# Weight rounding in four evenly dealt pieces, weight sums on VectorE, and another product order

## The chip, the cores and the metric

The kernel runs on one core of one Trainium2 chip. TensorE (PE in the profile) does the matrix products, VectorE (DVE) and ScalarE (ACT) the work on single elements, GpSimd (POOL) a little of it and the stores, and SyncE (SP) issues the loads. The metric is the device time of one execution in microseconds.

## What is computed

Attention inside chunks of 64 tokens, then a gated layer, then a layer with a rational function. All matrices are 32-bit floats.

```python
scores = scale * q_c @ k_c.T; attn = softmax(scores)        # 4 x 8 heads, 9 chunks of 64, head size 64
x = (attn @ v_c).reshape(2304, 512)
y = ((x @ w_a) * (x @ w_b)) @ w_out                          # 512 -> 1536 -> 512
h = y @ w_in
P = a[0] + a[1] * h + a[2] * h * h + a[3] * h * h * h
Q = 1 + abs(b[0]) * abs(h) + abs(b[1]) * h * h
out = (P / (Q + 1e-6)) @ w_out2                              # 512 -> 2048 -> 512
```

## The kernel before

**Numbers in two parts.** A matrix product takes both operands as a high and a low part: `mm3` (line 226) multiplies high by high, high by low and low by high into one place of PSUM. So every operand has to be split first: ACT rounds it to the high part, DVE subtracts to get the low one. For weights the split is longer, because a weight is first rounded in a particular way. `w_front` (line 187) takes a raw weight tile of 128x512 and makes a term c with two DVE instructions (lines 199, 200) and a term z with two ACT instructions (lines 201, 202). `w_next` (line 205) adds them on DVE (line 216), then `w_put` makes the high part on ACT (line 184) and, one call later through `w_flush`, the low part on DVE (line 185). That is four DVE and three ACT instructions for each tile. There are 24 tiles of w_a and w_b, 12 of w_out, and 32 of w_in and w_out2. `w_fetch` (line 154) loads them, `AHEAD` = 5 tiles early in the first stage and 2 early later.

**The order.** The order of every engine's instructions is that in which the Python code calls them; each engine works its own list from the front, and an instruction that waits holds all behind it. A list `todo` with due times (`later`, `tick`, line 245) strews the attention's pieces between the products.

**A start** (to 26.6 us): the attention of the first three units of 128 tokens, in an order written by hand (`FIRST`, `LOADS`, lines 80 and 83).

**The first stage** (26.6 to 200.1 us): `ab_half` (line 460) forms x @ w_a and x @ w_b of the first 768 tokens, 24 pairs (`seq`, line 784) of two times 12 products of 384 columns, 576 in all. Between them stand the attention of the other 15 units and the weights: `w_more` (line 792) makes one or no weight after each half pair. A unit's softmax (`a_soft`, line 345 ends it) is followed by a transposition on PE (line 353). After six units `x_second` (line 410) makes the differences that the second stage needs, on POOL (lines 399 and 417).

**The second stage** (200.1 to 432.9 us): x @ w_a and x @ w_b of the other 1536 tokens with seven instead of eight block products. `s_prep` (line 488) makes the sums of the weights for a tile i of 12: it takes the rounded weights back from memory (`s_load`, line 481, one buffer `wf`), forms four sums on POOL (line 512) and splits on ACT and DVE (lines 503 and 507). `s_step` (line 538) runs one tile over 768 tokens, 24 steps of 42 products of 384 columns. A step's order on PE is product 1, 2, then 7 of the step before, 5, 6, then 3 of the step before, then 4. After product 7 ACT copies y (`s_snap`, line 535), DVE forms `b` from it and from the sum q (line 576), and only then may product 3 add to q.

**The third stage** (432.9 to 623.4 us): `y_part` (line 614) multiplies with w_out, 60 places of 12 products: 12 places of 256 columns and 48 of 512. `g_fetch` loads a place's operand two places ahead, `g_parts` (line 608) splits it one place ahead (ACT line 116, DVE line 117). The 32 weights of the last stage are rounded here too, by `w_next` behind each place.

**The fourth stage** (623.4 us to the end): the layer with the rational function, `step2`.

Of the kernel before, what the change touches and what calls it, by code (L numbers as in the profile page):

```python
# [11 lines left out]
I32 = mybir.dt.int32  # L12
# [8 lines left out]
def chunk_attention_two_mlps(  # L21
# [104 lines left out]
    p_qk = phase.enter_context(tc.tile_pool(name="qk", bufs=2, side="right"))  # L126
    p_t = phase.enter_context(tc.tile_pool(name="t", bufs=5, side="right"))
# [20 lines left out]
    raws = {}  # L148

    n_cv = [0, 0, len(order1)]  # L150
    pend_w = []
    front_w = []
# [29 lines left out]
    def w_put(key, x):  # L182
        wt[key] = hi, lo = w_tile(key, F32R)
        nc.scalar.copy(hi, x)
        return lambda: nc.vector.tensor_tensor(lo, x, hi.bitcast(F32), ALU.subtract)  # L185

    def w_front():

        while n_cv[0] < n_cv[2] and n_cv[0] < n_cv[1] + (AHEAD if n_cv[0] < len(order1) else 2):
            w_fetch()  # L190
        if n_cv[1] == n_cv[2]:
            return
        t = raws.pop(order[n_cv[1]])
# [3 lines left out]
        c, z = w_tile(order[n_cv[1]], I32)  # L197
        zz = z.bitcast(F16).rearrange("p (f t) -> p f t", t=2)
        nc.vector.tensor_scalar(c.bitcast(F32), hw.bitcast(F32), 2.0 ** -112, None, ALU.mult)
        nc.vector.tensor_scalar(c, c, 3, None, ALU.logical_shift_left)  # L200
        nc.scalar.activation(zz[:, :, 1], hw.bitcast(F32), AF.Copy, scale=2.0 ** -112)  # L201
        nc.scalar.activation(zz[:, :, 0].bitcast(U16), lw, AF.Copy, scale=2.0 ** -13)  # L202
        front_w.append((c, z))

    def w_next(n):


        for _ in range(min(n, n_cv[2] - n_cv[1])):
            if not front_w:
                w_front()  # L210
            c, z = front_w.pop()
            key = order[n_cv[1]]
            n_cv[1] += 1
            x = p_io.tile([P, DM], I32, name="w_x", tag="io")
            w_flush()
# [3 lines left out]
            pend_w.append(w_put(key, x.bitcast(F32)))  # L219
            w_front()  # L220

    def w_flush():
        if pend_w:
            pend_w.pop()()
# [235 lines left out]
    def ab_half(i, h, nm):  # L460
        ps = ps_acc.tile([P, GH], F32, name="ab", tag="acc")
        for kk in range(KD):
            if kk == KD // 2:
                tick(0.5)
# [14 lines left out]
    wf = {}  # L479

    def s_load(i):

        t = p_j2.tile([P, 4, 2 * P], F32, name="wf", tag="wf")
# [4 lines left out]
    def s_prep(i):  # L488
# [4 lines left out]
        n = 2 * P  # L493

        p = p_j2 if i % 2 == 0 else p_j1
        made = {}

        def hi(nm, at, m, products):
            def f():
                t = made[nm] = (p if nm in "ab" else p_j1).tile([P, 2, m], F32R, name="ws_" + nm, tag=f"ws_{nm}{i % 2}")  # L500
# [29 lines left out]
    def s_tile(name):  # L530
        return p_j1.tile([P, GH], F32, name=name, tag=name, bufs=2)
# [6 lines left out]
    def s_step(i, g, prev, fill):  # L538
# [18 lines left out]
        if i is not None:  # L557
# [5 lines left out]
            fill()  # L563
        last()
# [43 lines left out]
    def g_parts(j, i):  # L608
        hi = p_g.tile([P, SIZES[j]], F32R, name="g_hi", tag="g_hi")
        lo = p_g.tile([P, SIZES[j]], F32R, name="g_lo", tag="g_lo")  # L610
        split(hi, lo, raw.pop(("g", j, i)))
        g1[j, i] = (hi, lo)

# [151 lines left out]
    for item in FIRST:  # L765
        if item in "fwl":
            w_front() if item == "f" else w_flush() if item == "l" else w_next(1)
            continue
# [15 lines left out]
    seq = [(i, h) for h in range(2) for i in range(3)] + [(i, h) for i in range(3, F1) for h in range(2)]  # L784
    for n in range(UH):
        a_unit(UH + n, 0.5 * n, (0, 0.5, 1, 1.5, 2, 3, 4))
    FROM, PER, GAP = 5.5, 3.0, 2.0
    for n in range((NQ - 1) * 2 * UH):
        a_unit(2 * UH + n, FROM + PER * n + (GAP if n >= 2 * UH else 0), (0, 0.5, 2, 3, 3.5, 5, 6.5))
    slot = 0  # L790
    for n, (i, h) in enumerate(seq):
        def w_more():
            due = min(slot + 3, 6) if slot < 6 else slot // 2 + 4
            if min(due, len(order1)) > n_cv[1]:
                w_next(min(due, len(order1)) - n_cv[1])
            else:
                w_flush()

# [3 lines left out]
        w_more()  # L802
        tick(0.5)
        slot += 1
        ps_b = ab_half(i, h, "b")
        if n == len(seq) - 1:
            break
        gated(i, h, a_s, ps_b)
        w_more()
        tick(0.5)  # L810
        slot += 1
    w_flush()
    phase.close()

    p_j1 = phase.enter_context(tc.tile_pool(name="j1", bufs=1, side="right", reuse_waits="tile"))
# [114 lines left out]
```

## Time and profile before

| | us |
|---|---|
| median of 3 runs | 1020.22 (1019.73 to 1023.4) |
| the profiled execution's own time | 1022.57 |
| its span in the trace | 1020.8 |
| PE busy | 932.6 (91%) |
| DVE busy | 725.3 (71%) |
| ACT busy | 590.5 (58%) |
| POOL busy | 143.8 (14%) |

The page gives each engine's busy time, the granted clock of TensorE in slices of the span, the groups of instructions with what ended the idle time ahead of them, and the DMA issues. A matmul's end is modelled, so its listed length overlaps the next one; how fast products really follow each other is read from their starts. The mean granted clock over the span is 0.958 of full speed.

### The profile page before, as it was taken

The page shows a single profiled execution, that of the slowest core. Times are in us where ns is not written, and L with a number is a line of the kernel's source. Part 1 is how long each engine was busy: PE and PEld are TensorE (multiplying, and loading weights), DVE is VectorE, ACT ScalarE, POOL GpSimd, SP SyncE. Part 2 cuts the span into 40 slices and gives each one's busy share as a digit, 9 for nine tenths or more (in the row PEclk, how much of TensorE's full clock was granted, in tenths as well). Part 3 has the DMA queues.
Part 4 walks back from the last instruction along what each step waited for, and adds up shares of the span by engine and source line. Part 5 has one row for each costly group of instructions (what it writes and reads, how often), then busy time and mean ns, then how long its engine had stood idle before and what let it go on. Part 6 is the DMA issues. An engine that isn't in the chain of part 4 may idle for free.

```text
span 1020.8 us, 14783 instructions
## 1 busy us (share of the span) xinstructions
PE 932.6 (91%) x5516; PEld 812.7 (80%) x5516; DVE 725.3 (71%) x1286; ACT 590.5 (58%) x1070; POOL 143.8 (14%) x192
## 2 busy tenths in 40 slices
PE   6689979978888799968999989999999999999998
PEld 5579978868888699866666669988888888888897
DVE  5567868545547576646556555999988988898896
ACT  5456756334223343335555546888767766776775
POOL 0011363372232232200000000000000000000000
PEclk9789989979789999989999999999999999999999
DMA  9948866223222323265666552002002000200100
GB/s 231 247 131 251 243 172 157 73 78 132 90 81 80 120 90 117 72 200 183 206 204 218 205 175 83 1 1 73 0 1 83 1 1 1 73 1 1 42 1 31
DMA packets 107335, 105.82 MB, mean 104 GB/s; under 512 B 61440, under 2 KB 84480, under 8 KB 107264
## 3 DMA queue, kind: packets, MB, share of 16 engines
q1 hardware_dynamic: 99264, 79.71, 27.1%
q0 software_dynamic: 8000, 25.17, 6.8%
q8 instruction: 43, 0.70, 0.3%
q14 instruction: 28, 0.23, 0.1%
HBM read 74.98 MB, written 29.88 MB: 103 GB/s over the span
## 4 chain that ended last, share of the span: by engine, by line
PE 44%; ACT 5%; DVE 3%; issue 2%; DMA 1%; ACTq 0%; SPq 0%
PE acc L229 8%; PE acc L230 8%; PE acc L228 8%; PE h L230 6%; PE h L228 6%; PE h L229 6%; ACT g_hi L116 1%; DVE g_lo L117 1%; DVE w_x L216 1%; DMA g_raw<-g_d 1%; ACT w_i L201 1%; ACT w_i L202 1%; DVE w_o L185 1%; ACT w_o L201 1%; DVE w_i L185 1%
## 5 line engine op out<-in xcount | busy, mean ns | idle before, releaser
L230 PE MATMUL h<-y,w_i 128*128 128x512 f32 (+1 forms) x320 | 117.8, 368 | 0.0
L228 PE MATMUL h<-y,w_i 128*128 128x512 f32 (+1 forms) x320 | 117.8, 368 | 0.0
L229 PE MATMUL h<-y,w_i 128*128 128x512 f32 (+1 forms) x320 | 117.7, 368 | 0.0
L228 PE MATMUL acc<-g_hi,w_o 128*128 128x512 f32 (+1 forms) x240 | 93.4, 389 | 16.7 <-ACT g_hi L116 16.7
L229 PE MATMUL acc<-g_lo,w_o 128*128 128x512 f32 (+1 forms) x240 | 93.8, 391 | 5.7 <-DVE g_lo L117 5.3
L677 ACT ACTIVATE a_ring<-h 128x512 f32<-128x512 f32 (+1 forms) x80 | 44.1, 551 | 89.3 <-PE h L230 89.3
L230 PE MATMUL acc<-g_hi,w_o 128*128 128x512 f32 (+1 forms) x240 | 91.4, 381 | 0.0
L117 DVE TENSOR_TENSOR g_lo<-g_raw,g_hi 128x512 fp32r<-128x512 f32 (+1 forms) x60 | 37.8, 638 | 73.0 <-ACT g_hi L116 72.8
L680 DVE SCALAR_TENSOR_TENSOR u<-u,cb_t,a_ring 128x512 f32<-128x512 f32 (+1 forms) x80 | 55.7, 696 | 31.2 <-ACT u L678 30.4
L229 PE MATMUL acc<-w_o,g_hi 128*128 128x512 f32 x191 | 75.2, 394 | 0.0
L228 PE MATMUL acc<-w_o,g_hi 128*128 128x512 f32 x191 | 74.8, 392 | 0.0
L230 PE MATMUL acc<-w_o,g_lo 128*128 128x512 f32 x191 | 74.2, 388 | 0.0
L228 PEld LDWEIGHTS acc<-g_hi,w_o 128*128 128x128 f32 x240 | 47.2, 197 | 31.4 <-ACT g_hi L116 23.4
L535 ACT COPY s<-y 128x384 f32<-128x384 f32 x72 | 34.1, 476 | 64.8 <-PE y L230 63.9
L470 POOL DMA_DIRECT2D g_d<-g x72 | 39.6, 550 | 224.4 <-DVE g L579 93.5
L228 PEld LDWEIGHTS h<-y,w_i 128*128 128x128 f32 x320 | 60.1, 188 | 9.0
L229 PEld LDWEIGHTS h<-y,w_i 128*128 128x128 f32 x320 | 60.1, 188 | 8.7
L230 PEld LDWEIGHTS h<-y,w_i 128*128 128x128 f32 x320 | 60.0, 188 | 7.5
L229 PEld LDWEIGHTS acc<-g_lo,w_o 128*128 128x128 f32 x240 | 47.2, 197 | 20.8 <-DVE g_lo L117 12.8
L228 PE MATMUL q<-xs,ws 128*128 128x384 f32 x96 | 36.1, 377 | 25.6 <-DVE b L576 25.4
L679 ACT ACTIVATE t<-h,ca_t 128x512 f32<-128x512 f32 (+1 forms) x80 | 59.0, 738 | 0.0
L682 DVE SCALAR_TENSOR_TENSOR t<-t,ca_t,h 128x512 f32<-128x512 f32 (+1 forms) x80 | 55.6, 694 | 2.8
(167 smaller groups left out, 2563.1 us busy)
## 6 DMA issues: line engine op xcount, KB each, us to landing
w_raw<-in_moe_w_out_dram SPq DMA_DIRECT2D x28, 512.0 KB, 3.8
g_d<-g POOLq DMA_DIRECT2D x72, 192.0 KB, 2.2
g_raw<-g_d SPq DMA_DIRECT2D x48, 256.0 KB, 3.9
w_raw<-in_moe_w_in_dram SPq DMA_DIRECT2D x16, 512.0 KB, 3.8
w_raw<-in_moe_w_a_dram SPq DMA_DIRECT2D x12, 512.0 KB, 6.0
w_raw<-in_moe_w_b_dram SPq DMA_DIRECT2D x12, 512.0 KB, 5.7
out_dram<-o SPq DMA_DIRECT2D x18, 256.0 KB, 2.4
y_d<-ys POOLq DMA_DIRECT2D x16, 256.0 KB, 4.2
```

What stands on the lines that cost most here:

```text
L117: nc.vector.tensor_tensor(lo, x, hi.bitcast(F32), ALU.subtract)
L185: return lambda: nc.vector.tensor_tensor(lo, x, hi.bitcast(F32), ALU.subtract)
L201: nc.scalar.activation(zz[:, :, 1], hw.bitcast(F32), AF.Copy, scale=2.0 ** -112)
L228: nc.tensor.matmul(ps, wh, xh, start=first, stop=False, **kw)
L229: nc.tensor.matmul(ps, wh, xl, start=False, stop=False, **kw)
L230: nc.tensor.matmul(ps, wl, xh, start=False, stop=last, **kw)
L470: nc.gpsimd.dma_start(out=g_d[i][:, tok:tok + GH], in_=g)
L535: nc.scalar.copy(t, ps)
L677: nc.scalar.activation(ah, ps, AF.Abs)
L679: nc.scalar.activation(t, ps, AF.Identity, scale=ca_t[:, 3:4], bias=ca_t[:, 2:3])
L680: nc.vector.scalar_tensor_tensor(u, u, cb_t[:, 0:1], ah, ALU.add, ALU.mult)
L682: nc.vector.scalar_tensor_tensor(t, t, ca_t[:, 1:2], ps, ALU.add, ALU.mult)
```

## The change

**Weights.** `w_front`, `w_next` and `w_put` become `w_piece`: four pieces, each with one DVE instruction and, save the last, one ACT instruction; a weight's high part is made in the second piece of the next weight and its low part in the third. `w_until` is called at every half of a product group (`half`), so the pieces come two at a time at first and then singly; in the second stage about 2.3 stand in each step; in the third stage `g_parts` hands back its DVE instruction, which is issued behind the first piece. One weight fewer is loaded ahead.

**Sums.** The four sums of each tile move from POOL to DVE. `wf` gets two buffers and is loaded two tiles ahead. The sums of tiles 0 and 1 are loaded, and those of tile 0 made, within the first stage (`s_begin`, at due time `END`), whose attention units follow each other a little faster. The split sums lie in the space of x and of the raw weights, which are free by then.

**Products.** Product 4 of a step stands ahead of product 3 of the step before.

```diff
     FIRST = (
-        "k0 d2 q0 k1 q1 S0 X0 d4 S1 X1 k2 E0 f q2 E1 P0 S2 V0 d2 P1 X2 L0 w V1 E2 k3 q3 l L1 d2 P2 V2 L2 w"
+        "k0 d2 q0 k1 q1 S0 X0 d4 S1 X1 k2 E0 w w q2 E1 P0 S2 w w V0 d2 P1 X2 L0 w w V1 E2 w w L1 d2 P2 w w V2 L2 w"
     ).split()
-    LOADS = "k0 q0 k1 q1 w v0 k2 q2 w v1 v2 w k3 q3 w k4 q4 v3 w k5 q5 v4 v5".split()
-
-    AHEAD = 5
+    LOADS = "k0 q0 k1 q1 w v0 k2 q2 w v1 v2 w k3 q3 w k4 q4 v3 k5 q5 v4 v5".split()
+
+    AHEAD = 4
...
+        if piece == 0:
+            nc.scalar.activation(zz[:, :, 1], hw.bitcast(F32), AF.Copy, scale=2.0 ** -112)
+            nc.vector.tensor_scalar(c.bitcast(F32), hw.bitcast(F32), 2.0 ** -112, None, ALU.mult)
+        elif piece == 1:
+            w_hi(n - 1)
+            nc.vector.tensor_scalar(c, c, 3, None, ALU.logical_shift_left)
+        elif piece == 2:
+            nc.scalar.activation(zz[:, :, 0].bitcast(U16), lw, AF.Copy, scale=2.0 ** -13)
+            w_lo(n - 1)
+            w_fetch_ahead(n + 1)
+        else:
+            del terms[n]
+            x = f32s[n] = p_io.tile([P, DM], I32, name="w_x", tag="io")
             nc.vector.tensor_tensor(x, c, z, ALU.add)
...
-        t = p_j2.tile([P, 4, 2 * P], F32, name="wf", tag="wf")
+        t = p_j2.tile([P, 4, 2 * P], F32, name="wf", tag="wf", bufs=2)
...
         def add(o, x, y, op):
-            return lambda: nc.gpsimd.tensor_tensor(f[:, o], f[:, x], f[:, y], op)
+            return lambda: nc.vector.tensor_tensor(f[:, o], f[:, x], f[:, y], op)
 
         return [
-            hi("a", 0, 2 * n, (1, 2)), lo("a", 0, 2 * n), hi("b", 3 * n, n, (4,)), lo("b", 3 * n, n),
+            hi("a", 0, 2 * n, (1, 2)), hi("b", 3 * n, n, (4,)), lo("a", 0, 2 * n), lo("b", 3 * n, n),
             add(3, 2, 3, ALU.add), add(2, 0, 2, ALU.subtract), add(0, 3, 0, ALU.subtract),
-            hi("2", 2 * n, 2 * n, (7, 5)), lo("2", 2 * n, 2 * n), add(1, 1, 0, ALU.subtract),
-            hi("1", 0, 2 * n, (6, 3)), lo("1", 0, 2 * n),
+            hi("2", 2 * n, 2 * n, (7, 5)), add(1, 1, 0, ALU.subtract), hi("1", 0, 2 * n, (6, 3)),
+            lo("2", 2 * n, 2 * n), lo("1", 0, 2 * n),
         ]
...
             s2 = s_snap(y, "s2")
             fill()
+            r = ps_ab.tile([P, GH], F32, name="r", tag="ab"[n % 2])
+            s_product(r, i, g, 4, True)
+            fill()
         last()
         fill()
         if i is None:
             return None
-        r = ps_ab.tile([P, GH], F32, name="r", tag="ab"[n % 2])
-        s_product(r, i, g, 4, True)
-        fill()
...
-    seq = [(i, h) for h in range(2) for i in range(3)] + [(i, h) for i in range(3, F1) for h in range(2)]
+    seq = [(i, h) for h in range(2) for i in range(4)] + [(i, h) for i in range(4, F1) for h in range(2)]
     for n in range(UH):
-        a_unit(UH + n, 0.5 * n, (0, 0.5, 1, 1.5, 2, 3, 4))
-    FROM, PER, GAP = 5.5, 3.0, 2.0
+        a_unit(UH + n, 1.0 + 0.5 * n, (0, 0.5, 1.5, 2, 2.5, 3.5, 4.5))
+    FROM, PER, GAP = 6.0, 2.75, 1.0
...
+    def s_begin():
+
+        nonlocal p_j2
+        s_t.close()
+        p_j2 = s_t.enter_context(tc.tile_pool(name="j2", bufs=1, side="right", reuse_waits="tile"))
+        s_load(0)
+        s_load(1)
+
+    def s_do(t, op):
+        if op == 0:
+            preps[t] = s_prep(t)
+        preps[t][op]()
+        if op == 11 and t + 2 < F1:
+            s_load(t + 2)
+
+    END = math.ceil(2 * (FROM + PER * ((NQ - 1) * 2 * UH - 1) + GAP + times[-1] + 0.25)) / 2
+    todo.append((END, n_todo[0], s_begin))
...
+        n = n_half[0]
+        n_half[0] += 1
+        w_until(min(11 + 2 * n, 32) / 4 if n < 17 else (n + 18) / 4)
...
     for n, (j, i) in enumerate(places):
         if n + 2 < len(places):
             g_fetch(*places[n + 2])
+        due = done + (4 * len(order2) * spent[n] // spent[-1] if n < len(spent) else 4 * len(order2))
+        due -= n_cv[1]
+        low = lambda: None
         if n + 1 < len(places):
-            g_parts(*places[n + 1])
+            low = g_parts(*places[n + 1])
+        if due:
+            w_piece()
+        low()
+        for _ in range(due - 1):
+            w_piece()
         y_part(j, i)
         evacuate(1)
-        due = -(-len(order2) * spent[n] // spent[-1]) if n < len(spent) else len(order2)
-        w_next(due + len(order1) + len(ordero) - n_cv[1])
```

On PE, in the middle of the second stage, `y<-xs` are the last products 6 of a step, `q<-xs` is product 3 of the step before and `r<-xs` product 4. Before:

```order
L229 MATMUL y<-xs,ws_4090 128x384
L230 MATMUL y<-xs,ws_4090 128x384
L228 MATMUL q<-xs,ws_3931 128x384
L229 MATMUL q<-xs,ws_3931 128x384
L230 MATMUL q<-xs,ws_3931 128x384
L228 MATMUL q<-xs,ws_3931 128x384
L229 MATMUL q<-xs,ws_3931 128x384
L230 MATMUL q<-xs,ws_3931 128x384
L228 MATMUL r<-xs,ws_b 128x384
```

The same place on PE now (`j_x` is the space that the split sums lie in):

```order
L245 MATMUL y<-xs,j_x 128x384
L246 MATMUL y<-xs,j_x 128x384
L244 MATMUL r<-xs,j_x 128x384
L245 MATMUL r<-xs,j_x 128x384
L246 MATMUL r<-xs,j_x 128x384
L244 MATMUL r<-xs,j_x 128x384
L245 MATMUL r<-xs,j_x 128x384
L246 MATMUL r<-xs,j_x 128x384
L244 MATMUL q<-xs,j_x 128x384
```

The six products r now stand between the products 6 and the products q.

On ACT, in the second stage at the start of a new tile's sums, `s<-y` are the copies of y (the second one below is the one that `b` needs), `ws_a` and `ws_b` the splits of the freshly loaded `wf`. Before:

```order
L503 CAST ws_3454<-wf 128x512
L535 COPY s<-y 128x384
L503 CAST ws_a<-wf 128x512
L535 COPY s<-y 128x384
L503 CAST ws_b<-wf 128x256
L535 COPY s_3517<-y 128x384
```

The same place on ACT now:

```order
L220 ACTIVATE w_o_28_3370<-w_raw 128x512
L572 COPY s<-y 128x384
L540 CAST ws_a<-wf 128x512
L540 CAST j_x<-wf 128x256
L572 COPY s<-y 128x384
L572 COPY s_3493<-y 128x384
```

Both splits of `wf` now stand ahead of the copy, where one did, and the `wf` they read was asked for two tiles earlier.

On ACT, in the third stage, `g_hi` is the split of a place's operand, `w_o` and `w_i` are weights, `ys` a result that is written out. Before:

```order
L116 CAST g_hi<-g_raw 128x512
L626 COPY ys<-acc 128x512
L184 CAST w_i_6_48_5227<-w_x 128x512
L201 ACTIVATE w_o_6_49_5231<-w_raw 128x512
L202 ACTIVATE w_o_6_49_5231<-w_raw 128x512
L116 CAST g_hi<-g_raw 128x512
```

The same place on ACT now:

```order
L649 CAST g_hi<-g_raw 128x512
L191 CAST w_o_5_47_5206<-w_x 128x512
L220 ACTIVATE w_i_6_48_5183<-w_raw 128x512
L665 COPY ys<-acc 128x512
L649 CAST g_hi<-g_raw 128x512
L214 ACTIVATE w_o_6_49_5236<-w_raw 128x512
L191 CAST w_i_6_48_5240<-w_x 128x512
L649 CAST g_hi<-g_raw 128x512
```

Between two splits stand one or two weight instructions where there were three or none, and the high part (line 191) belongs to a weight whose sum was formed a piece earlier.

## Rows read from the trace of the kernel before

**Rows 1.** stages: length, busy and count of PE, PEld, DVE, ACT, POOL; PEclk, DMA share, GB/s

```profile
0.00:26.64 26.64, 16.91 (x256) 14.23 (x256) 13.67 (x37) 13.74 (x26) 1.39 (x7) 0.94 1.08 229
26.64:200.10 173.46, 155.21 (x1708) 141.90 (x1708) 118.25 (x241) 99.68 (x190) 51.75 (x60) 0.93 0.68 185
200.10:432.90 232.80, 198.63 (x1010) 190.57 (x1009) 138.15 (x239) 82.42 (x162) 79.19 (x105) 0.90 0.28 95
432.90:623.40 190.50, 168.35 (x731) 130.69 (x732) 105.71 (x198) 101.08 (x179) 9.53 (x19) 0.96 0.58 190
623.40:1020.80 397.40, 393.54 (x1813) 335.32 (x1812) 349.48 (x574) 293.56 (x513) 1.90 (x4) 1.00 0.07 24
```

**Rows 2.** waits of PE: reader <- releaser, us in total, times, longest

```profile
PE q L228 <- DVE b L576: 25.4, 10, 4.2
PE acc L228 <- ACT g_hi L116: 16.7, 17, 4.3
PE at L353 <- DVE e L345: 6.8, 3, 4.4
PE at L306 <- ACT kT L308: 5.5, 1, 5.5
...
PE ab L230 <- DVE w_b L185: 2.7, 1, 2.7
```

**Rows 3.** timeline of PE, second stage: start, length, line [idle before, releaser]

```profile
271.11 0.34 PE L229 MATMUL y<-xs,ws 128*128 128x384 f32 x1
...
273.36 0.34 PE L230 MATMUL y<-xs,ws 128*128 128x384 f32 x1
277.03 0.69 PE L228 MATMUL q<-xs,ws 128*128 128x384 f32 x1 [3.33 <-DVE b L576]
...
278.16 0.52 PE L228 MATMUL q<-xs,ws 128*128 128x384 f32 x1
278.48 0.52 PE L229 MATMUL q<-xs,ws 128*128 128x384 f32 x1
...
297.56 0.69 PE L228 MATMUL q<-xs,ws 128*128 128x384 f32 x1 [3.11 <-DVE b L576]
```

**Rows 4.** timeline of SP, same stretch

```profile
272.53 0.32 SPq L485 DMA_DIRECT2D wf<-w_a  x1
```

**Rows 5.** timeline of ACT, same stretch

```profile
275.39 0.62 ACT L503 CAST ws_a<-wf 128x512 fp32r<-128x512 f32 x1 [3.24 <-DMA wf<-w_a]
275.91 0.47 ACT L535 COPY s<-y 128x384 f32<-128x384 f32 x1
```

**Rows 6.** busy time in 25 us of full-rate steps, columns of Rows 1

```profile
375.00:400.00 25.00, 24.28 (x140) 23.96 (x140) 19.31 (x36) 11.19 (x22) 10.26 (x16) 1.00 0.29 98
```

**Rows 7.** forms on DVE: count | busy, mean ns of one | idle before

```profile
L185 DVE TENSOR_TENSOR w_i<-w_x,w_i 128x512 fp32r<-128x512 f32 x16 | 10.9, 684 | 0.0
...
L507 DVE TENSOR_TENSOR ws_b<-wf,ws_b 128x256 fp32r<-128x256 f32 x12 | 5.0, 418 | 0.1
```

**Rows 8.** timeline of POOL, first stage

```profile
134.47 1.84 POOL L417 TENSOR_TENSOR x<-x 128x768 f32<-128x768 f32 x1
```

**Rows 9.** timeline of DVE, the same moment

```profile
134.64 2.23 DVE L185 TENSOR_TENSOR w_a<-w_x,w_a 128x512 fp32r<-128x512 f32 x1
```

**Rows 10.** timeline of ACT, first stage, the wait for a table of coefficients

```profile
37.15 0.20 ACT L779 ACTIVATE cb_t<-cb_t 128x2 f32<-128x2 f32 x1 [7.43 <-DMA cb_t<-in_moe_b_dram]
```

**Rows 11.** timeline of PE, third stage, products of 512 columns

```profile
465.09 0.39 PE L230 MATMUL acc<-g_hi,w_o 128*128 128x512 f32 x1
...
466.49 0.39 PE L230 MATMUL acc<-g_hi,w_o 128*128 128x512 f32 x1
```

**Rows 12.** a wait of ACT over the span, columns of Rows 2

```profile
ACT w_o L184 <- DVE w_x L216: 52.6, 27, 3.2
```

**Rows 13.** DMA issues on the page: size of one, us from issue to landing

```profile
g_raw<-g_d SPq DMA_DIRECT2D x48, 256.0 KB, 3.9
...
y_d<-ys POOLq DMA_DIRECT2D x16, 256.0 KB, 4.2
```

More of the change, by code (lines that the diff above doesn't have):

```diff
@@ L180, in w_tile, with w_fetch_ahead @@
         return t[:, 0], t[:, 1]
[L182 to L189, printed above, removed]
-            w_fetch()
-        if n_cv[1] == n_cv[2]:
-            return
-        t = raws.pop(order[n_cv[1]])
+    def w_fetch_ahead(n):
+        while n_cv[0] < n_cv[2] and n_cv[0] < n + (AHEAD if n_cv[0] < len(order1) else 2):
+            w_fetch()
@@ new lines, in w_hi, with w_lo, w_piece @@
+    def w_hi(n):
+        if n in f32s:
+            key = order[n]
+            wt[key] = w_tile(key, F32R)
+            nc.scalar.copy(wt[key][0], f32s[n].bitcast(F32))
+    def w_lo(n):
+        if n in f32s:
+            hi, lo = wt[order[n]]
+            nc.vector.tensor_tensor(lo, f32s.pop(n).bitcast(F32), hi.bitcast(F32), ALU.subtract)
+    def w_piece():
+        n, piece = divmod(n_cv[1], 4)
+        n_cv[1] += 1
+        key = order[n]
+        if piece == 0:
+            w_fetch_ahead(n)
+            t = raws.pop(key)
+            terms[n] = (t, *w_tile(key, I32))
+        t, c, z = terms[n]
@@ L203, in w_front @@
[L203 to L215, printed above, removed]
+        if piece == 0:
+            nc.scalar.activation(zz[:, :, 1], hw.bitcast(F32), AF.Copy, scale=2.0 ** -112)
[10 more added lines that the diff above has]
+            x = f32s[n] = p_io.tile([P, DM], I32, name="w_x", tag="io")
@@ L218, in w_next, with w_until @@
                 nc.gpsimd.dma_start(out=w1_d[key], in_=x.bitcast(F32))
-            pend_w.append(w_put(key, x.bitcast(F32)))
-            w_front()
+    def w_until(tiles):
+        while n_cv[1] < min(4 * tiles, 4 * n_cv[2]):
+            w_piece()
     def w_flush():
-        if pend_w:
-            pend_w.pop()()
+        n = n_cv[1] // 4 - 1
+        if n in f32s:
+            w_hi(n)
+            w_lo(n)
     def mm3(ps, w, x, first, last, **kw):
@@ L463, in ab_half @@
             if kk == KD // 2:
-                tick(0.5)
+                half()
             x = [t[:, kk, h * GH:(h + 1) * GH] for t in (x_hi, x_lo)]
@@ L479, in chunk_attention_two_mlps, with j_room @@
     wf = {}
+    j_x = {}
+    J_AT = {"20": 0, "21": 1, "10": 2, "11": 3, "a1": 4, "b": 5}
+    def j_room(nm):
+        t, at = divmod(J_AT[nm], 3)
+        if ("j", t) not in j_x:
+            j_x["j", t] = p_x0.tile([P, 3, 2, DM], F32R, name="j_x", tag=f"x_{('hi', 'lo')[t]}")
+        return j_x["j", t][:, at]
     def s_load(i):
-        t = p_j2.tile([P, 4, 2 * P], F32, name="wf", tag="wf")
+        t = p_j2.tile([P, 4, 2 * P], F32, name="wf", tag="wf", bufs=2)
         for n, nm in enumerate("ab"):
@@ L493, in s_prep, with place @@
         n = 2 * P
-        p = p_j2 if i % 2 == 0 else p_j1
         made = {}
+        def place(nm):
+            if nm == "a" and i % 2 == 0:
+                return p_j2.tile([P, 2, DM], F32R, name="ws_a", tag="ws_a")
+            at = {"20": 8, "10": 9, "a1": 10, "b0": 11, "b1": 11}.get(f"{nm}{i}")
+            if nm == "b":
+                if at not in j_x:
+                    t = j_room("b") if at is None else p_w.tile([P, 2, DM], F32R, name="ws_b", tag=f"w{at}")
+                    j_x[at] = t.rearrange("p a f -> p (a f)").rearrange("p (i a f) -> p i a f", i=2, a=2)
+                return j_x[at][:, i % 2]
+            if at:
+                return p_w.tile([P, 2, DM], F32R, name="ws_" + nm, tag=f"w{at}")
+            return j_room(f"{nm}{i % 2}")
         def hi(nm, at, m, products):
             def f():
-                t = made[nm] = (p if nm in "ab" else p_j1).tile([P, 2, m], F32R, name="ws_" + nm, tag=f"ws_{nm}{i % 2}")
+                t = made[nm] = place(nm)[:, :, :m]
                 for x, c in enumerate(products):
@@ L530, in s_tile @@
     def s_tile(name):
-        return p_j1.tile([P, GH], F32, name=name, tag=name, bufs=2)
+        return p_j2.tile([P, GH], F32, name=name, tag=name, bufs=2)
     def s_snap(ps, name="s"):
@@ L610, in g_parts @@
         lo = p_g.tile([P, SIZES[j]], F32R, name="g_lo", tag="g_lo")
-        split(hi, lo, raw.pop(("g", j, i)))
+        x = raw.pop(("g", j, i))
+        nc.scalar.copy(hi, x)
         g1[j, i] = (hi, lo)
+        return lambda: nc.vector.tensor_tensor(lo, x, hi.bitcast(F32), ALU.subtract)
     def y_part(j, i):
@@ L844, in fill @@
         for t, op in plan.get((step, m), ()):
-            if op == 0:
-                preps[t] = s_prep(t)
-            preps[t][op]()
-            if op == 11 and t + 1 < F1:
-                s_load(t + 1)
-        if m == 4 and step >= 2:
-            w_next(-(-(step - 1) * len(ordero) // 22) + len(order1) - n_cv[1])
+            s_do(t, op)
+        if (step, m) == (1, 3):
+            w_fetch_ahead(len(order1))
+        if step >= 2 and (7 * step + m) % 3 == 0:
+            w_until(min(n_cv[1] + 1, 4 * n_cv[2]) / 4)
         tick(0.5)
@@ L872, in chunk_attention_two_mlps @@
     n_cv[2] += len(order2)
+    w_fetch_ahead(len(order1) + len(ordero))
     places = [(j, i) for j in range(NB) for i in range(F1)]
-    spent = [sum(SIZES[j] for j, _ in places[:n + 1]) for n in range(len(places) - 4)]
+    spent = [max(0, sum(SIZES[j] for j, _ in places[:n + 1]) - 2 * SIZES[0]) for n in range(len(places) - 4)]
+    done = n_cv[1]
     a_ring = None
```

73 lines of the change are left out of this document (32 added, 41 removed).

## Prediction

> **What bounds the kernel now.** I read the stages first, then PE's waits, then the timelines around the longest of them. The stages [rows 1] show that PE is the engine to watch: it is busy for most of every stage, but in the fourth it has no gap worth naming and a granted clock of 1.00, while in the second and third it is idle for 34.2 and 22.2 us and its clock is 0.90 and 0.96. Two fifths of the span are thus full of products already (397.4 us, and nothing of the change reaches into them), and what can be won lies in the 597 us between 26.6 and 623.4.
>
> The waits [rows 2] say where. The largest, 25.4 us in ten pieces, is product 3 of the second stage waiting for `b` on DVE. Reading it as "DVE is slow" would be wrong. The timelines go one step further back. Products of 384 columns follow each other in (273.36 - 271.11) / 13 = 0.173 us; then PE stands for 3.33 us and goes on at 0.32 us a product, which is the lower of the clock's two levels [rows 3]. Meanwhile SP asked for the next tile's `wf` only at 272.53 [rows 4], and ACT's split of that tile, the last instruction ahead of the copy of y, stood for 3.24 us for its landing [rows 5]. The copy is what `b` needs. So a load that is asked too late holds ACT's queue, ACT holds DVE, DVE holds PE, and the idle time costs clock as well: from one such wait to the next are 20.53 us for two steps of 42 products, which take 84 x 0.173 = 14.5 at the full rate. 6.0 us are lost each time, 3.1 to 3.3 by waiting and 2.7 to 2.9 by the clock.
>
> In the third stage PE waits 16.7 us for `g_hi` on ACT [rows 2], and ACT in turn waits 52.6 us in 27 pieces over the span for a weight's sum on DVE [rows 12]: whole weights in ACT's queue stand ahead of the operand's split.
>
> **The change, stage by stage.** The sum is made against the profiled execution: 1022.57 us, of which 1020.8 are the span. Its own time lies 2.35 us above the median of the runs, and I take that off at the end.
>
> *Second stage, now 232.8 us.* It has 24 x 42 = 1008 products, 174.4 us at 0.173. Lost are 58.4, which is what ten waits of 6.0 come to. With two buffers `wf` is asked for when the tile two back is finished, a whole pair of steps (14.5 us) ahead of its use instead of 2.9 us (272.53 to 275.39), so the wait on ACT should be gone. Product 3 comes six products (1.04 us) later, which makes 18 products or 3.1 us between products 7 and 3; the chain that must fit is the copy (0.47, [rows 5]), DVE's `b` (384 of 512 columns' 0.684, so 0.51, [rows 7]) and handing over, about 1.3. What is late next is then DVE's queue: it is busy 19.31 us in 25 us that hold 140 products [rows 6], which is 5.8 us in a step of 7.27. The four sums of a tile, two in a step, add something that the trace does not show on DVE. Nearest is a subtraction of the same size there, 0.418 us [rows 7]; from below they could cost 0.34, half of the 0.684 of a subtraction twice as wide [rows 7], from above 2 us, if each is held as the instruction at 134.64 was: 2.23 us instead of the 0.684 that its form takes elsewhere [rows 7, 9], beside an operation on POOL of 1.84 us [rows 8]. I take 0.42, because with the sums gone POOL has nothing but stores left in the steps from the third on. That is 0.84 in a step, 6.6 of 7.27: full, but below the product time. In steps 0 and 1 POOL still makes the differences of x, so there I reckon with the other end: eight sums of tiles 0 and 1 at 1.5 us more, half of it hidden, some 4 us at PE with its clock. The last step has no products between 7 and 3 and keeps its wait of a good 1 us. The seam to the first stage disappears, since tile 0 is prepared before. 174.4 + 4 + 1.5 = 180, a gain of 52.5; from 25 (the wait only shrinks) to 58.
>
> The Trainium skill, SBUF — State Buffer, section "Who interferes with whom", says that an operation of DVE with two inputs in SBUF and one of GpSimd that reads SBUF exclude each other for the whole instruction, the later one blocking. The pair at 134.5 agrees [rows 8, 9]. By that rule alone every sum and split of tiles 0 and 1 could be held, 16 at about 1.5 us, and the stage would keep some 10 us more than I say; from step 2 on the rule speaks for the change.
>
> *Third stage, now 190.5 us.* The spacing at 512 columns is (466.49 - 465.09) / 6 = 0.233 us [rows 11]. 48 x 12 of these are 134.4; 144 of half the width 16.8 by proportion; 12 of the fourth stage's first products 2.1: 153.3. Lost are 37. With single pieces the split of a place's operand follows at once when its buffer is free, takes 0.62 on ACT and 0.68 on DVE at that width [rows 5, 7], and has 12 x 0.233 = 2.8 us for it: hidden. What is late next are transfers. SP's loads of weights wait for a raw tile to be read, and the next operand's load stands behind them; at 256 columns a place lasts only 1.4 us against 3.9 from issue to landing [rows 13], so I leave 6 us there. At each of four block ends a result is written (4.2) and its buffer loaded anew (3.9), 8.1 together [rows 13], with six buffers for about 2.6 takers a place, 6.4 us: 1.7 us each, 7. And 2 for the start. 153.3 + 15 = 168, a gain of 22; from 5 (transfers bound it) to 33.
>
> *First stage, now 173.5 us.* PE's wait for a low part of a weight, 2.7 us [rows 2], should go, since a weight is done two pieces ahead of its use and eight tiles instead of six share the crowded beginning. The wait of 5.5 for a copy on ACT [rows 2] comes from ACT standing 7.43 us for a small table that is loaded behind everything else [rows 10]; one weight of 0.52 MB fewer ahead of it brings it 2.3 us forward at 229 GB/s [rows 1], and 3.2 stay. Of the 6.8 for the softmax, 4.4 in one piece fall where POOL holds DVE [rows 2, 8, 9]; nothing takes that away, I count 2.4 as gone at most and take 2. Together 7; the clock's mean of 0.93 over 173.5 us is 12.1 us lost beside 18.3 of idle time [rows 1], so each us of waiting takes 0.65 along: 12, and 2 for the denser attention, which ends sooner. A gain of 14. New here is that two pieces stand in each half at the beginning, and a late piece holds the next weight; if it does, the stage gains nothing, if the clock recovers wholly it gains 22.
>
> *Sum.* 52.5 + 22 + 14 = 88.5. 1022.6 - 88.5 = 934, less 2.35 for the median: 932 us.
>
> **Rivals.**
> (a) The late load is not the cause of product 3's wait, and only the 1.04 us that product 4 gives are won. For it speaks that the profile names DVE; against it the order of rows 3 to 5. The second stage gains 10 x 1.04, and about 10 with the clock and the seam: 20 instead of 52.5, total 964.
> (b) The third stage was held by transfers all along and stays as it is: 954. Against it, its waits are put down to ACT and DVE, and not one to a load [rows 2].
> (c) Slower: DVE's queue becomes the bound of the second stage. Everything ahead of `b`, a weight's piece or a sum, delays product 3 as soon as more than 3.1 - 1.3 = 1.8 us of it are in front. 6.6 of 7.27 us leave little room, and a queue that full runs late easily. If every step then waits as those ten did, 24 x 6.0 = 144 over 174.4 make a stage of 318: 85.5 us longer, less the 36 of the other stages, and the kernel takes 1070. Against it, at the full rate DVE showed 77% without any of PE's waits in [rows 6], and the sums fall behind `b` in most steps.
> (d) The evenly dealt pieces only move the waits (each piece now crosses from ACT to DVE by itself) and all stages give back what they gain: about 1020.
>
> **Chances.** The forecast 0.72, its own range 915 to 950; (a) 0.10, (b) 0.10, (c) 0.05, (d) 0.03. The range 908 to 968 takes in (a), (b) and the best ends of all stages but one, and leaves (c), (d) and the tails. Half a per cent, 5 us, is about what can be told from no change. Faster: the forecast, (a), (b) and a third of (d), 0.93; the same 0.02; slower 0.05.
>
> **What would show it.** Right: no wait of ACT for `wf` in the second stage, products 3 following at 0.173 us, its clock near 1.00 and its length near 180; waits for `g_hi` nearly gone and a third stage near 168; the fourth unchanged at 397. Wrong: PE's waits for `b` again in every step, with DVE busy over 95% of a step (then (c)), or in every other step with ACT behind a load (then (a)); a third stage above 180 with ACT waiting for `g_raw` (then (b)); a first stage of 173 or more with PE waiting for weights' parts.

## The result and the profile after

The changed kernel takes 959.08 us (median of four runs, 956.45 to 963.04), the kernel before on the same chip 1020.46: a ratio of 0.940 (95% interval 0.936 to 0.944). It is faster by 61 us where 88.5 were forecast, so 27 are missing. The time lies outside the forecast's own range of 915 to 950, and inside the wider one of 908 to 968 that also takes in two rivals. The profiled execution took 956.45 us, its span is 954.7, and the mean granted clock is 0.977 of full speed (0.958 before).

The stages of the changed kernel, each from its first product to the next one's (the fourth from its first product behind the third's last); the columns are those of [rows 1]:

```profile
0.00:26.86 26.86, 17.86 (x249) 14.69 (x249) 15.03 (x40) 14.29 (x27) 2.06 (x8) 0.82 1.07 229
26.86:196.74 169.88, 154.18 (x1716) 141.30 (x1717) 123.86 (x240) 101.99 (x194) 57.15 (x62) 0.95 0.70 193
196.74:383.49 186.75, 180.09 (x1010) 178.74 (x1009) 150.59 (x285) 81.82 (x158) 35.82 (x53) 0.97 0.35 119
383.49:557.30 173.81, 163.44 (x733) 128.30 (x733) 106.17 (x198) 102.62 (x181) 10.14 (x19) 0.98 0.61 202
557.30:954.70 397.40, 393.51 (x1813) 335.32 (x1811) 349.39 (x574) 293.51 (x513) 1.87 (x4) 1.00 0.07 24
```

Cut in the same way, by first products, the stages of the kernel before are 26.6, 174.8, 230.9, 191.1 and 397.4 us (the cuts of [rows 1] lie up to 1.4 us from these). So the second stage gives 44.1, the third 17.3, the first 4.9, and the fourth nothing.

The length of a stage in a single profile has a spread of its own, and the experiments below give it, since most of them leave a stage as it was. The second stage repeats to 0.02 us in the four profiles in which its code and what runs beside it are the same. From the start to the end of the first stage it is 196.5 to 200.3 us in eight profiles with the new code (mean 198.2), 200.1 to 202.0 in three with the old (201.2). The third stage is 173.8 to 181.0 in eight with the new code (176.8), 190.2 to 191.1 in three with the old (190.5). The profile shown above is thus a lucky one, and the typical gains are 3 us up to the end of the first stage, 44 in the second and 14 in the third. They come to 61, as the medians do.

The waits of PE in the changed kernel, to be held against [rows 2]:

```profile
PE acc L245 <- DVE g_lo L651: 5.0, 13, 2.1
PE at L322 <- ACT kT L324: 5.0, 1, 5.0
PE acc L244 <- ACT g_hi L649: 4.9, 7, 2.0
PE at L322 <- DMA kqv<-in_k_dram: 4.4, 1, 4.4
PE at L339 <- ACT x L396: 4.3, 1, 4.3
PE q L244 <- ACT ws L540: 3.2, 1, 3.2
PE at L386 <- DMA w_raw<-in_moe_w_b_dram: 3.2, 1, 3.2
PE at L369 <- DVE e L361: 3.1, 2, 2.6
PE y L246 <- DVE ws_a L544: 2.3, 1, 2.3
...
PE q L244 <- DVE b L613: 1.2, 1, 1.2
```

Product 3's wait for `b` went from 25.4 us in ten pieces to one piece of 1.2, the one in the last step. The waits for `g_hi` went from 16.7 to 4.9 us; those for the low part `g_lo` beside it are as long as before. In the first stage the wait for a weight's low part is gone and those for the softmax are halved, but two others have grown. Three waits of PE in the kernel before, which stand now at 5.0 (`g_lo`), 4.3 (line 339) and 3.2 us (line 386):

```profile
PE acc L229 <- DVE g_lo L117: 5.3, 15, 2.1
...
PE at L370 <- DVE x_lo L390: 2.1, 1, 2.1
...
PE at L323 <- ACT x L380: 0.7, 1, 0.7
```

In the steps at full rate (25 us, columns as above) PE has no gap and DVE is busy 21.19 us, with 146 products where [rows 6] had 140 and 19.31:

```profile
275.00:300.00 25.00, 25.00 (x146) 25.00 (x145) 21.19 (x44) 12.16 (x24) 4.01 (x7) 1.00 0.38 136
```

SP asks for `wf` two tiles ahead, and ACT's copy of y waits for PE alone. First SP, then ACT, at the place that answers to [rows 4, 5]:

```profile
278.17 0.32 SPq L510 DMA_DIRECT2D wf<-w_a  x1
```

```profile
279.72 0.62 ACT L540 CAST ws_a<-wf 128x512 fp32r<-128x512 f32 x1
280.24 0.41 ACT L540 CAST j_x<-wf 128x256 fp32r<-128x256 f32 x1
281.43 0.48 ACT L572 COPY s<-y 128x384 f32<-128x384 f32 x1 [0.78 <-PE y L246]
```

### The profile page after: what moved, and what is told of

Same layout as the page of the kernel before. It is cut to its first block, busy times and chain, and to the rows that moved or that the text cites. A ratio compares the mean times of both kernels' runs of the same rounds, so it can differ in the third digit from the quotient of the medians.

```text
span 954.7 us, 14746 instructions
## 1 busy us (share of the span) xinstructions
PE 909.1 (95%) x5516; PEld 798.4 (84%) x5516; DVE 745.0 (78%) x1334; ACT 594.2 (62%) x1070; POOL 107.0 (11%) x144
## 4 chain that ended last, share of the span: by engine, by line
PE 74%; DMA 9%; ACT 6%; DVE 5%; SPq 4%; issue 2%; ACTq 0%; DVEq 0%
PE acc L245 8%; PE acc L246 8%; PE acc L244 8%; DMA g_raw<-g_d 7%; PE h L246 7%; PE h L244 7%; PE h L245 7%; PE ab L244 3%; PE ab L246 3%; PE ab L245 3%; PE y L246 3%; PE y L245 3%; PE y L244 3%; SPq L313 2%; PE q L244 2%
## 5 line engine op out<-in xcount | busy, mean ns | idle before, releaser
L716 ACT ACTIVATE a_ring<-h 128x512 f32<-128x512 f32 (+1 forms) x80 | 44.1, 551 | 88.8 <-PE h L246 88.8
L244 PE MATMUL acc<-g_hi,w_o 128*128 128x512 f32 (+1 forms) x240 | 91.7, 382 | 5.0 <-ACT g_hi L649 4.9
L246 PE MATMUL acc<-g_hi,w_o 128*128 128x512 f32 (+1 forms) x240 | 90.5, 377 | 0.0
L649 ACT CAST g_hi<-g_raw 128x512 fp32r<-128x512 f32 (+1 forms) x60 | 34.5, 575 | 63.2 <-DMA g_raw<-g_d 45.5
```

The lines of the kernel that those rows point to most:

```text
L244: nc.tensor.matmul(ps, wh, xh, start=first, stop=False, **kw)
L246: nc.tensor.matmul(ps, wl, xh, start=False, stop=last, **kw)
L716: nc.scalar.activation(ah, ps, AF.Abs)
```

## Experiments: what freed the second stage

The theory was that one load, asked for too late, holds ACT, ACT holds `b` and `b` holds product 3. The rivals were the order of the products, the place of the sums and the size of the weights' pieces. Three runs undo one part of the change each, two do one part alone in the kernel before, and two undo several. A run's ratio is to the kernel before as it was timed beside that run.

**The early load undone.**

```diff
-        t = p_j2.tile([P, 4, 2 * P], F32, name="wf", tag="wf", bufs=2)
+        t = p_j2.tile([P, 4, 2 * P], F32, name="wf", tag="wf", bufs=1)
...
-        s_load(1)
...
-        if op == 11 and t + 2 < F1:
-            s_load(t + 2)
+        if op == 11 and t + 1 < F1:
+            s_load(t + 1)
```

> The changed kernel with the load of the sums' input as before: one buffer wf, asked for behind the last subtraction of the tile before. Theory (a load asked too late holds ScalarE, ScalarE holds b on VectorE, b holds product 3): ScalarE waits again 2 to 4 us for wf once in every tile, product 3 waits for b behind it, and the second stage grows from 186.8 us to between 215 and 245, the time to between 988 and 1018. Rival (the six products that now stand ahead of product 3 are what freed it, the load is hidden anyway): the second stage stays under 192 us, the time under 965.

Measured: 960.77 us, 0.944 (0.940 to 0.948) of the kernel before; second stage 188.4 us. The expectation of the theory failed, and that of the rival held. The waits of ACT and then of PE in this stage:

```profile
ACT j_x L540 <- DMA wf<-w_a: 11.6, 5, 3.4
...
ACT ws_a L540 <- DMA wf<-w_a: 9.5, 5, 2.7
```

```profile
PE q L244 <- DVE b L613: 2.7, 3, 1.3
```

ACT does wait again for `wf`, 21.1 us in ten pieces, but that no longer reaches PE. Something else takes it up.

**The product order undone.** The call of product 4 goes back behind `last()`.

```diff
-            r = ps_ab.tile([P, GH], F32, name="r", tag="ab"[n % 2])
-            s_product(r, i, g, 4, True)
-            fill()
         last()
         fill()
         if i is None:
             return None
+        r = ps_ab.tile([P, GH], F32, name="r", tag="ab"[n % 2])
+        s_product(r, i, g, 4, True)
+        fill()
```

> The changed kernel with product 4 behind product 3 of the step before, as it was. Theory of the late load: the copy, b and the handing over take 1.3 us, 12 products of 384 columns 2.08, so product 3 hardly waits and the second stage grows by 0 to 5 us, the time to between 957 and 965. Rival (product order is the cause): product 3 waits in most steps for b, about 1 us each with the clock falling too, the stage grows by 20 to 40 us, the time is 980 to 1000.

Measured: 959.68 us, 0.943 (0.939 to 0.948); second stage 185.7 us, 1.0 less where the theory had 0 to 5 more. With the load in time the order gains nothing.

**The sums back on GpSimd.**

```diff
-            return lambda: nc.vector.tensor_tensor(f[:, o], f[:, x], f[:, y], op)
+            return lambda: nc.gpsimd.tensor_tensor(f[:, o], f[:, x], f[:, y], op)
```

> The changed kernel with the four sums of each tile back on GpSimd (0.74 us each there, 0.42 on VectorE in the changed kernel's steady steps). Theory: VectorE is held while GpSimd adds, so 11 tiles give 4 x 0.74 = 3 us each in which VectorE's subtractions may stand, but the steps have 18 products between products 7 and 3; the stage grows by 3 to 15 us, the time to between 962 and 975. Rival 1 (the sums' engine does not matter once the load is early): within 3 us of the changed kernel. Rival 2 (VectorE is the fuller engine, so relieving it helps): 3 to 6 us faster than the changed kernel.

Measured: 962.12 us, 0.945 (0.940 to 0.950); second stage 187.6 us, 0.8 more where the theory had 3 to 15. Rival 1 held: which engine adds hardly matters there.

**The product order alone, in the kernel before.** Its edit is the one of the change.

> The kernel before with one edit: product 4 ahead of product 3 of the step before. Theory of the late load: each of the ten waits of product 3 loses the 1.04 us of six products and a little clock, and ScalarE still waits about 3 us for wf; 10 to 20 us are gained, time 1000 to 1010. Rival (product order is the cause): the waits for b vanish, the second stage goes from 232.8 to about 185 us, time 970 to 980.

Measured: 1005.37 us, 0.987 (0.982 to 0.993); second stage 216.2 us, 14.7 less, as the theory had it. ACT still waits for `wf` in ten places (33.5 us), and PE for `b`:

```profile
PE q L228 <- DVE b L576: 18.8, 10, 2.8
```

**The early load alone, in the kernel before.**

```diff
-        t = p_j2.tile([P, 4, 2 * P], F32, name="wf", tag="wf")
+        t = p_j2.tile([P, 4, 2 * P], F32, name="wf", tag="wf", bufs=2)
...
     s_load(0)
+    s_load(1)
...
-    s_load(1)
+    s_load(2)
...
-            if op == 11 and t + 1 < F1:
-                s_load(t + 1)
+            if op == 11 and t + 2 < F1:
+                s_load(t + 2)
```

> The kernel before with one edit: two buffers wf, loaded two tiles ahead. Theory of the late load: ScalarE's waits of 3.2 us for wf and product 3's for b go, the second stage goes from 230.9 us to between 190 and 200, the time to 980 to 990. Rival 1 (what holds the copy is a queue full of whole weights and sums; a load in time is only one of several things late there): product 3 still waits 1 to 2 us in most tiles, the stage ends between 205 and 220. Rival 2 (the load does not matter, as its undoing alone in the changed kernel cost nothing): the stage stays above 225.

Measured: 984.56 us, 0.968 (0.964 to 0.972); second stage 199.1 us, 31.8 less. The theory's numbers held here: with the old order, whole weights and the sums on GpSimd, the load in time leaves two waits for `b` and none of ACT for `wf`:

```profile
PE q L228 <- DVE b L576: 3.7, 2, 2.6
```

**Load and order undone together.** The two edits above in one kernel.

> The changed kernel with both undone, the late load and product 4 behind product 3; each alone cost less than 2 us of the second stage. Theory (they cover for each other: ScalarE is still 1.5 to 3.4 us late with the late load, and the six products ahead of product 3 take it up): product 3 waits for b in most tiles, 1 to 2 us, the stage goes from 186.8 us to between 195 and 212, the time to between 967 and 985. Rival (the weights' pieces, dealt evenly, are what freed ScalarE's and VectorE's queues): the stage stays under 191 us.

Measured: 982.59 us, 0.966 (0.962 to 0.970); second stage 206.6 us, 19.8 more, where each edit alone cost +1.7 and -1.0. Ten waits are back:

```profile
PE q L244 <- DVE b L613: 16.7, 10, 2.4
```

So the two parts cover for each other: a load that is late by up to 3.4 us on ACT is taken up by the six products that now stand ahead of product 3, and with a load in time they have nothing to take up.

**Load, order and the weights' pieces undone together.**

```diff
-        if step >= 2 and (7 * step + m) % 3 == 0:
-            w_until(min(n_cv[1] + 1, 4 * n_cv[2]) / 4)
+        if m == 4 and step >= 2:
+            w_until(len(order1) - (-(step - 1) * len(ordero) // 22))
```

> The changed kernel with the late load, the old product order, and in the second stage whole weights (four pieces together, in the fifth gap of a step) in place of single pieces. With the first two undone the stage took 206.6 us, the kernel before 230.9. Theory (the rest of the difference is the weights: three of ScalarE's and four of VectorE's instructions in one go stand ahead of the split of wf and of the copy): the stage goes to between 214 and 230, the time to between 988 and 1005. Rival (the rest is GpSimd's sums and the start of the stage, where the first tile was not prepared before): the stage stays between 203 and 210.

Measured: 997.01 us, 0.978 (0.974 to 0.983); second stage 222.5 us, 15.9 more than with the pieces:

```profile
PE q L244 <- DVE b L613: 24.5, 10, 3.4
```

That is [rows 2]'s 25.4 again. Whole weights lengthen the waits that the late load makes. What makes the 8.4 us that are left to the 230.9 was not tested: the sums on GpSimd, the start of the stage and the places of the sums within a step are still different.

## Experiments: where the missing 27 us are

**Whole weights in the third stage.**

```diff
-        due = done + (4 * len(order2) * spent[n] // spent[-1] if n < len(spent) else 4 * len(order2))
-        due -= n_cv[1]
-        low = lambda: None
         if n + 1 < len(places):
-            low = g_parts(*places[n + 1])
-        if due:
-            w_piece()
-        low()
-        for _ in range(due - 1):
-            w_piece()
+            g_parts(*places[n + 1])()
         y_part(j, i)
         evacuate(1)
+        due = -(-len(order2) * spent[n] // spent[-1]) if n < len(spent) else len(order2)
+        w_until(done // 4 + due)
```

> The changed kernel with the weights of the third stage made whole, four pieces together behind each place, as before; nothing else. Theory (whole weights in ScalarE's queue stand ahead of the operand's split): TensorE waits again about 15 us for g_hi, and the third stage goes from 173.8 us back to 185 to 192, the time to between 970 and 978. Rival (the stage got shorter because of its loads, one raw weight fewer in the way, and the pieces do nothing): the stage stays within 4 us of 173.8.

Measured: 979.58 us, 0.961 (0.957 to 0.966); third stage 194.6 us, over the expected 185 to 192 and a little longer than before. PE's waits for the split are back:

```profile
PE acc L244 <- ACT g_hi L649: 19.1, 20, 2.2
```

Without the pieces, and the low part's place between them, nothing is left of what the third stage gained.

**The third stage's weights loaded by another queue.** In the kernel before ACT waited in this stage for the weights' sums on DVE (57.6 us) and hardly for the operand (2.7 us). In the changed kernel it waits for the operand, and SP, which asks for it, waits for a raw weight tile to be read. ACT's row first, then SP's:

```profile
ACT g_hi L649 <- DMA g_raw<-g_d: 45.5, 29, 3.2
```

```profile
SPq L169 <- ACT w_o L220: 38.2, 14, 4.5
SPq L169 <- ACT w_i L220: 28.9, 14, 4.3
```

The edit lets GpSimd's queue, which has only the stores to do, ask for the raw weights:

```diff
-        nc.sync.dma_start(out=dst, in_=src)
+        (nc.sync if at < len(order1) + len(ordero) else nc.gpsimd).dma_start(out=dst, in_=src)
```

> The changed kernel with the raw weights of the third stage asked for on GpSimd's queue and not on SyncE's, where the loads of the operand g_raw stand behind them. Theory (the rest of the third stage's loss is SyncE standing for a raw tile to be read, 67 us of waits on ScalarE's second activation, while g_raw waits behind): ScalarE's 45.5 us of waits for g_raw shrink to under 20, and the stage goes from 173.8 us to 160 to 168, the time to between 945 and 953. Rival (the transfers themselves, or the write and reload of results at the ends of blocks, set it): the stage stays within 3 us of 173.8.

Measured: 948.47 us, 0.931 (0.926 to 0.935); third stage 163.4 us. ACT's wait for the operand is nearly gone, with the same bytes from the same places:

```profile
ACT g_hi L649 <- DMA g_raw<-g_d: 4.6, 4, 1.4
```

A weight's load takes longer on that queue (5.2 and 4.8 us from issue to landing for the two kinds, against 3.9 and 3.6), and the stage is shorter all the same. So the loss was neither transfer time nor the ends of the blocks; it was a queue that stood for one thing with another behind it. The Trainium skill, DMA: Bandwidth & Descriptors, section "Issuing engines are not separate DMA queues", says that starting transfers from several engines saves only the time that it takes to start them, which is usually small. The measurement differs where the starting engine itself stands in a wait: about 14 us of the stage were saved here.

**The wait for the coefficients put off.** In the changed kernel ACT stood 8.80 us for the table (7.43 in [rows 10]), and PE 5.0 us for a copy behind it.

```diff
-    nc.scalar.activation(cb_t, cb_t, AF.Abs)
...
+    todo.append((END, n_todo[0], lambda: nc.scalar.activation(cb_t, cb_t, AF.Abs)))
+    n_todo[0] += 1
     n_half = [0]
```

> The changed kernel with ScalarE's first use of the small table of coefficients put off from 36 us to the end of the first stage's attention. Theory (ScalarE stood 8.8 us for that table and TensorE 5.0 us for a copy behind it): the wait of 5.0 us is gone, the clock of the stretch 25 to 75 us rises a little, the first stage goes from 169.9 us to 162 to 166, the time to between 951 and 956. Rival (everything at that place waits for loads that arrive at the same time, 229 to 254 GB/s all along): another wait takes its place and the stage stays within 2 us.

Measured: 955.15 us, 0.938 (0.933 to 0.942), which can't be told from the changed kernel's 0.940 (0.936 to 0.944). ACT now stands at the next thing that is still on its way:

```profile
38.70 0.78 ACT L214 ACTIVATE w_a<-w_raw 128x512 f16<-128x512 f32 x1 [5.59 <-DMA w_raw<-in_moe_w_a_dram]
```

and PE waits 4.4 us instead of 5.0. The rival holds for the wait: another load takes its place. Its reason holds only in part: in the changed kernel the DMA share is 1.07 up to the first product of the stage, but 0.76, at 173 GB/s, while ACT stands there (27.5 to 36.3 us). The first stage ends at 194.8 us from the start, earlier than in the eight profiles above (196.5 to 200.3), so some 3 us may have been gained; one profile does not settle it.

**The differences of x on VectorE.**

```diff
-            lambda: nc.gpsimd.tensor_tensor(lo, x, hi.bitcast(F32), ALU.subtract),
+            lambda: nc.vector.tensor_tensor(lo, x, hi.bitcast(F32), ALU.subtract),
...
-            return lambda: nc.gpsimd.tensor_tensor(o, x, y, ALU.subtract)
+            return lambda: nc.vector.tensor_tensor(o, x, y, ALU.subtract)
```

> The changed kernel with the differences and low parts of x (22 operations of 128x768) on VectorE and not on GpSimd. Theory (VectorE is held by GpSimd's operations on the same memory; one of 0.17 us took 5.43 beside three of them): VectorE's instructions keep their usual lengths, TensorE's wait of 4.3 us at 146.6 us and the two of 3.2 and 2.3 us at the start of the second stage are gone, the first stage gains 3 to 6 us, the second 5 to 7, time 947 to 953. Rival (VectorE gets 22 x 1.0 us more work, in one queue with softmax and b, and delays both): the stages together stay within 3 us or grow.

Measured: 949.58 us, 0.933 (0.929 to 0.937). The second stage takes 177.9 us, 8.9 less, at a clock of 1.00, and PE's waits of 3.2 and 2.3 us at its start are gone. Its row, and then the rows of two forms on DVE in the first stage (count, busy, mean ns of one), of the changed kernel and of this one:

```profile
194.33:372.19 177.86, 175.70 (x1009) 174.75 (x1009) 143.48 (x287) 81.21 (x158) 26.03 (x47) 1.00 0.37 125
```

```profile
L196 DVE TENSOR_TENSOR w_b<-w_x,w_b 128x512 fp32r<-128x512 f32 x12 | 11.1, 928 | 1.5 <-ACT w_b L191 1.4
L359 DVE TENSOR_SCALAR s<-s 128x8 f32<-128x8 f32 x15 | 10.9, 723 | 0.5
```

```profile
L196 DVE TENSOR_TENSOR w_b<-w_x,w_b 128x512 fp32r<-128x512 f32 x12 | 8.2, 686 | 2.0 <-ACT w_b L191 2.0
...
L359 DVE TENSOR_SCALAR s<-s 128x8 f32<-128x8 f32 x15 | 2.6, 172 | 0.5
```

DVE has more to do now, and is busy for less: 121.1 us in the first stage against 123.9. The time that GpSimd held it was more than GpSimd's work costs on DVE (0.95 us for one of 128x768 there, 1.8 on GpSimd). PE's wait of 4.3 us became 2.7. The first stage ends at 194.3 us, and at 195.8 in the next run, which has the same edit; both are earlier than the eight profiles above, so that some 3 us may have been gained there too.

**Both gains in one kernel.** The last edit and the one of the queue together.

> The changed kernel with both edits that gained: the differences of x on VectorE, and the third stage's raw weights asked for on GpSimd's queue. If their gains add, as they lie in different stages: first and second stage as with the differences on VectorE (168 and 178 us), the third 10 us shorter, time between 935 and 943. Rival (the queue on GpSimd costs or the third stage is bound elsewhere once its start is early): 943 to 948.

Measured: 935.98 us (931.62 to 938.28), 0.920 (0.917 to 0.923) of the kernel before: faster than both kernels, and the gains add. Its second and third stage (POOL's column now holds the 32 issues of weights too):

```profile
195.81:373.67 177.86, 175.70 (x1010) 174.75 (x1009) 143.49 (x287) 81.07 (x158) 26.08 (x47) 1.00 0.35 119
373.67:536.60 162.93, 156.78 (x733) 127.97 (x733) 109.44 (x198) 104.25 (x181) 30.72 (x51) 0.99 0.70 222
```

## Why the prediction was right or wrong

*Direction and mechanism of the largest gain: right; the total in part luck.* 959 us is not what the forecast's own mechanism gave (915 to 950). It lies nearest to the totals of rivals (a) and (b), 964 and 954, and neither of these happened: three stages each gained less than reckoned, for reasons of their own.

The late load was the largest cause of the second stage's loss, shown by the load alone in the kernel before (-31.8 us). Rival (a), that the load is not the cause, is refuted by the same run. Rivals (c) and (d) did not come: DVE is busy 21.19 of 25 us, which is 21.19 x 42 / 146 = 6.1 us a step where 6.6 were reckoned, and PE never waits for it in the steady steps.

*Second stage: forecast 180, measured 186.8; the gain 52.5 was 44.1.* The term that failed is "some 4 us at PE" for DVE held by GpSimd in steps 0 and 1. It is 8.9 us, by the run that took GpSimd's operations away, which brought the stage to 177.9. I had reckoned with eight sums and half of the delay hidden, which by my own 1.5 us each is 6 and not 4. The splits of tiles 0 and 1 are held too; DVE's row for one of tile 1, then GpSimd's in that time:

```profile
204.68 6.35 DVE L544 TENSOR_TENSOR ws_a<-wf,ws_a 128x512 fp32r<-128x512 f32 x1
```

```profile
205.10 1.83 POOL L433 TENSOR_TENSOR x<-x 128x768 f32<-128x768 f32 x1
206.88 3.59 POOL L415 TENSOR_TENSOR xs<-x,xs 128x768 fp32r<-128x768 f32 x2
```

The split takes 0.68 us when it is alone. The rule of the Trainium skill that I weighed (SBUF — State Buffer, section "Who interferes with whom"), taken by itself, gave some 190; the measurement lies nearer to it than to my 180.

*What I credited to one cause has several.* I read all ten waits, 6.0 us each, as the load's. The load alone gives 31.8 us of the 44.1; the order alone would have given 14.7, and with a late load and the old order the pieces give 15.9. These don't add, because each shortens the same waits. What the other 12.3 us of the gain are made of was not told apart. Undoing a single part of the change therefore showed next to nothing, and the first of these runs came out 27 us under the near end of what I expected.

*Third stage: forecast 168, measured 173.8, 176.8 as the mean of eight; the gain 22 was 14 to 17.* That single pieces clear ACT's queue was right (whole weights bring the stage to 194.6). Wrong was the price of SP's queue. I had named the mechanism (loads of weights wait for a raw tile, the operand's load stands behind them) and left 6 us for it, for the 256-column places alone. It holds in the whole stage (41.1 of ACT's 45.5 us come after 408 us, where the places have 512 columns) and costs 13.6 us (176.8 - 163.2, the mean of the two runs without it). Rival (b), that transfers bind the stage, is refuted: with the same bytes it fell to 163. Half of the sign that I had named for it, ACT waiting for `g_raw`, did come (45.5 us): a slow transfer and one that is asked for late look alike there.

*First stage: the gain 14 was 3, or 4.9 in the profile shown.* The wait for a weight's low part, 2.7 us, is gone as forecast. Two things failed. The term for the table of coefficients gave 0.5 us at PE (5.5 to 5.0) where 2.3 were counted: with one weight fewer ahead of it ACT goes on only 0.9 us earlier (at 36.28 instead of 37.15), and its own wait grew from 7.43 to 8.80, since it is there sooner. The run that put it off shows that the wait is no lever: there ACT stands until 38.70 for a raw weight. And I had no term for waits that grow. The waits for the softmax shrank from 6.8 to 3.1 us, more than the 2 that I counted, but those of 0.7 and 2.1 us became 4.3 and 3.2. Behind the 4.3 is ACT's copy, which stood 6.20 us for operations on GpSimd. PE's idle time in the stage fell by 3.8 us (from 19.5 to 15.7) in the profile shown, where I reckoned with 7, and that leaves the factor of 1.65 for the clock little to work on.

*Fourth stage and start: unchanged, as forecast* (397.4; 26.9 against 26.6).

*The size of the error.* By typical stages 88.5 - 61 splits into 11 (first), 8 (second) and 8 (third). The last two had a held engine and a queue as their cause. Taking these away gave 8.9 and 13.6 us, the second more than was missing. That the kernel with both edits, at 936 us, lies within 4 of the 932 forecast for the change itself is therefore luck: the greater part of the first stage's 11 us is still missing.

## What to carry to other kernels

When a wait's chain ends in a late load, ask also what else in the chain has room to take it up: parts of a change that shorten one and the same wait cover for each other, so undo them together, or do one alone in the old kernel, before calling any of them useless. When a load seems slow, look first at what the engine that asks for it was waiting for. A second engine that works on the same memory can cost more than its work would cost on the first.

## What the runs showed of the hardware that was not expected

An operation on 128x8 numbers, 0.17 us by itself, took 5.43 us on DVE while GpSimd ended the issue of a store and then ran three operations one behind the other. DVE's row, then GpSimd's:

```profile
144.30 5.43 DVE L359 TENSOR_SCALAR s<-s 128x8 f32<-128x8 f32 x1
```

```profile
143.79 0.54 POOL L486 DMA_DIRECT2D g_d<-g  x1
144.34 1.81 POOL L415 TENSOR_TENSOR xs<-x,xs 128x768 fp32r<-128x768 f32 x1
146.10 1.81 POOL L433 TENSOR_TENSOR x<-x 128x768 f32<-128x768 f32 x1
147.87 1.83 POOL L415 TENSOR_TENSOR xs<-x,xs 128x768 fp32r<-128x768 f32 x1
```

It did not get in between them; it ended when the third did, at 149.7, although its record begins 0.04 us before the first. With the differences on VectorE the 15 operations of this form took 0.17 us on average. And it has a single tensor as input, where I had looked only at operations with two. The Trainium skill, SBUF — State Buffer, section "Who interferes with whom", counts this form among those that can take the pair of ports shared with GpSimd, under conditions on its operands. That several operations in a row keep it out is what this trace adds; whether the store's issue was what kept it out at first is not shown.
